# A two-layer MoE kernel: the operand sums of its last matrix product move from two engines to accumulating DMAs

## The chip, the cores and the metric

The kernel runs on one core of a Trainium2 chip. The metric is the device time of one execution, in microseconds (us). The core has a matrix engine (TensorE, PE), three engines for other arithmetic (VectorE, DVE; ScalarE, ACT; GpSimd, POOL), and SyncE (SP), which here issues transfers. Each engine takes its instructions in order. Transfers run on 16 DMA queues and may be issued from SP or POOL.

## What is computed

Attention over pooled keys and values gives `x`; two feed-forward layers follow, each with 4608 tokens, 512 model columns and 2048 inner columns:

```python
def reference(...):
    x = attn_out.transpose(0, 2, 1, 3).reshape(4608, 512)
    h = x @ moe_w_in;  x = maximum(0.01 * h, h) @ moe_w_out
    h = x @ moe2_w_in; g = where(h >= 1, h, where(h <= -1, 0, (h + 1)**2 / 4))
    return g @ moe2_w_out
# inside the attention: k and v are means over 8 rows, and
#   attn = exp(scores - max);  attn = attn / (sum(attn) + 1e-9)
```

All arrays are float32. The kernel keeps that accuracy by splitting each operand `a` into `hi` (rounded to the matrix engine's format) and `lo = a - hi`, and adding three products: hi x hi, hi x lo, lo x hi.

## The kernel before

The first layer runs in blocks of 512 tokens with the attention of later blocks woven in. The second layer's first product and its second product each use a Winograd form of Strassen's method: an operand is cut into 2 x 2 blocks, and 7 products of sums of blocks replace 8 products of blocks.

The change concerns the second product, `g @ moe2_w_out`, in `second_phase`. `g` lies in device memory, transposed, so that the inner dimension runs over partitions. A round `r` takes 1024 tokens (rounds 0 to 3; round 4 has 512) as two rows of 512 (256 in round 4), and the 2048 inner columns as two halves of 8 blocks `f`. So a block of `g` is `a11`, `a12`, `a21` or `a22`, each of 8 tiles `f` of 128 x 512. `g_load` brings them in by DMA from SP; the places are three sets of eight tiles, named `m0` to `m7`, `m8` to `m15` and so on in a listing of the program.

Within a round the seven products come in the order `ORDER2` = 4, 5, 7, 6, 1, 3, 2, each over the 8 blocks `f`. One product and one `f` is a *unit* `u`; a round has 56. A unit is 12 matmuls of 256 columns (4 groups of 128 tokens by 3), 6 in round 4. Four of the products need a sum, which `g_sum` makes in place, tile by tile: for 5, `a22 = a21 + a22`; for 7, `a21 = a11 - a21`; for 6, `a22 = a22 - a11`; for 3, `a22 = a12 - a22`. It puts even `f` on DVE and odd `f` on POOL (in round 4 all on POOL).

`hi(u)` is an ACT copy of the unit's operand and `lo(u)` a DVE subtraction. There are six pairs of tiles for them, so a pair comes free when PE has used the unit six before. The order of the work is written by hand: after the matmuls of unit `u` the program issues `hi(u + 5)`, `lo(u + 4)`, the sum for unit `u + 7`, in round 0 a fetch of product weights (`w2_fetch`, 512 KB for two `f`), the loads that reuse a place just read, and two steps of `post`. `post` copies or adds the banks of a finished product into output tiles and stores them; the additions of `q` to `r1` and `r2` there are POOL's.

Weights of the second product are split beforehand, in the first product's phase: `w2_sums` makes the sums of weight blocks on POOL, `w2_split` their `hi` (ACT) and `lo` (DVE), and a DMA puts them into device memory.

In the attention, `normalize` sums the exponentials over 64 columns and over 8 columns into two small tiles, adds them and 1e-9 with one DVE instruction, takes the reciprocal on DVE, and multiplies on POOL.

Of the kernel before, what the change touches and what calls it, by code (L numbers as in the profile page):

```python
# [17 lines left out]
P = 128  # L18
# [11 lines left out]
ORDER2 = (4, 5, 7, 6, 1, 3, 2)  # L30

# [4 lines left out]
def attention_moe_moe2(ctx: ExitStack, tc: tile.TileContext, qT, kT, v, k01, v01, w_in1, w_out1, w_in2, w_out2, out):  # L36
# [161 lines left out]
    class Attention:  # L198
        def __init__(self, apool):
            self.ap = apool  # L200
            self.sets = []
            for i in range(2):
                kp = apool.tile([P, KT, 2 * SP], F32, name=f"kp{i}", bufs=1)
                vh = apool.tile([P, KT, P], F32R, name=f"vh{i}", bufs=1)
                vl = apool.tile([P, KT, P], F32R, name=f"vl{i}", bufs=1)
                vr = apool.tile([96, KT, P], F32R, name=f"vr{i}", bufs=1)
                self.sets.append((kp, vh, vl, vr))
            self.q, self.main, self.rest, self.wide, self.raws = {}, {}, {}, {}, {}
            self.attn = {}
            self.u = None  # L210

        def zero(self):
            for kp, vh, vl, _ in self.sets:
                for t, n in ((kp, SP), (vh, D), (vl, D)):
                    nc.gpsimd.memset(t[0:64, :, n:].bitcast(F32), 0.0)
                    nc.gpsimd.memset(t[64:P, :, 0:n].bitcast(F32), 0.0)
            t = room(8, [P, 272], F32, "sums")
            self.sums = t[:, 0:176]
            self.sums_r = t[0:64, 176:272]
            nc.vector.memset(self.sums, 0.0)  # L220
            for c in (48, 112):
# [153 lines left out]
        def scores_early(self, blk, hf, ti, tag):  # L375
# [11 lines left out]
            m = self.ap.tile([P, 4, 1], F32, tag="stat", name=f"m{blk}_{hf}_{ti}", bufs=12)  # L387
# [16 lines left out]
            r = self.ap.tile([P, 4, 1], F32, tag="stat", name=f"r{blk}_{hf}_{ti}", bufs=12)  # L404
            r2 = self.ap.tile([P, 4, 1], F32, tag="stat", name=f"s{blk}_{hf}_{ti}", bufs=12)
# [6 lines left out]
        def scores(self, blk, hf, ti):  # L412
# [13 lines left out]
            m = self.ap.tile([P, 4, 1], F32, tag="stat", name=f"m{blk}_{hf}_{ti}", bufs=12)  # L426
# [4 lines left out]
            r = self.ap.tile([P, 4, 1], F32, tag="stat", name=f"r{blk}_{hf}_{ti}", bufs=12)  # L431
            r2 = self.ap.tile([P, 4, 1], F32, tag="stat", name=f"s{blk}_{hf}_{ti}", bufs=12)
# [6 lines left out]
        def normalize(self, n, main, rest, r, r2):  # L439
            nc.vector.tensor_reduce(out=r[0:n, :, 0], in_=main, axis=AX.X, op=ALU.add)  # L440
            yield True
            nc.vector.tensor_reduce(out=r2[0:n, :, 0], in_=rest, axis=AX.X, op=ALU.add)
            yield True
            nc.vector.scalar_tensor_tensor(
                out=r[0:n], in0=r[0:n], scalar=1e-9, in1=r2[0:n], op0=ALU.add, op1=ALU.add
            )
            yield True
            nc.vector.reciprocal(out=r[0:n], in_=r[0:n])  # L448
            yield True
            for t, w in ((main, MAIN), (rest, REST)):  # L450
                nc.gpsimd.tensor_tensor(out=t, in0=t, in1=r[0:n].to_broadcast([n, 4, w]), op=ALU.mult)  # L451
# [214 lines left out]
    class Second:  # L666
# [105 lines left out]
        def w2_sums(self, f):  # L772
# [6 lines left out]
            tt(out=s[:, 2], in0=b22, in1=b12, op=ALU.subtract)  # L779
# [3 lines left out]
        def w2_split(self, f, pos):  # L783
# [5 lines left out]
            self.parts(t[:, 0], t[:, 1], self.kept["w2s"][ORDER2[pos]])  # L789
# [217 lines left out]
        def g_sum(self, r, pos, f):  # L1007
            a = {w: self.a.get((r, w, f)) for w in ((1, 1), (1, 2), (2, 1), (2, 2))}
            prod = ORDER2[pos]
            tt = (nc.gpsimd if f % 2 or r == self.NPAIR2 - 1 else nc.vector).tensor_tensor  # L1010
            if prod == 5:
                tt(out=a[2, 2], in0=a[2, 1], in1=a[2, 2], op=ALU.add)
            elif prod == 7:
                tt(out=a[2, 1], in0=a[1, 1], in1=a[2, 1], op=ALU.subtract)
            elif prod == 6:
                tt(out=a[2, 2], in0=a[2, 2], in1=a[1, 1], op=ALU.subtract)
            elif prod == 3:
                tt(out=a[2, 2], in0=a[1, 2], in1=a[2, 2], op=ALU.subtract)
# [29 lines left out]
        def second_phase(self):  # L1048
# [5 lines left out]
            self.hi(4)  # L1054
            post = []
            for u, (r, pos, f) in enumerate(self.units):
# [17 lines left out]
                if u + 7 < NU:  # L1074
                    self.g_sum(*self.units[u + 7])
# [18 lines left out]
        def post(self, r, prod, n):  # L1094
# [17 lines left out]
            def snap(key, i, prod, row=None, col=None):  # L1112
                t = self.kept[key, r] = tile_of(i)
                yield
                for k in range(nb):
                    nc.scalar.activation(out=t[:, k], in_=banks(prod)[k], func=AF.Copy)
                    yield
                if row is not None:
                    store(t, row, col)

# [15 lines left out]
            def chain(*gens):  # L1136
# [9 lines left out]
                3: lambda: chain(add("q", 5, 0, 1)),  # L1146
                2: lambda: chain(snap("c11", 3, 1, 0, 0)),
# [256 lines left out]
```

## Time and profile before

| | |
|---|---|
| Median of 3 runs | 1707.95 us (1701.2 to 1708.09) |
| The profiled execution | 1704.4 us, of which the span in the profile is 1702.6 us |
| Mean granted TensorE clock | 0.991 of full speed |
| PE busy | 1660.0 us |
| DVE busy | 1086.4 us |
| ACT busy | 896.1 us |
| POOL busy | 448.0 us |
| Second product, first to last matmul | 1323.3 to 1698.8 us |

Times in the profile are microseconds from the start of the span. Busy times are sums over the whole span, and stages differ: what a stage waits for has to be read within the stage. The page's chain of waits goes back from the last instruction, at each step to what released it. "SPq" is SP issuing a transfer, which is not the time the transfer takes to land.

### The profile page before, as it was taken

To read this page: it belongs to the slowest core of one execution; us is meant where nothing else is said; L and a number is where in the kernel's file an instruction comes from. 1 tells how busy PE (TensorE), PEld (TensorE's weight loads), DVE (VectorE), ACT (ScalarE), POOL (GpSimd) and SP (SyncE) were. 2 spreads that over 40 slices of the span, in tenths; PEclk is the share of its full clock that TensorE was granted. 3 is DMA by queue.
4 is the path that set the end of the run, shared out by engine and by line. 5 is a ranking of instruction groups with operands and counts; after the bars stand their busy time and mean duration, and the time that the engine had idled before them with its cause. 6 is when DMAs were issued, how large, how long until landed. Compare 5 with 4: busy or idle time off the path is not lost.

```text
span 1702.6 us, 27338 instructions
## 1 busy us (share of the span) xinstructions
PE 1660.0 (97%) x9372; PEld 1478.9 (87%) x9372; DVE 1086.4 (64%) x2095; ACT 896.1 (53%) x1969; POOL 448.0 (26%) x552
## 2 busy tenths in 40 slices
PE   6889999999999999999999999999999799999998
PEld 4568878788888888888888899999999799999998
DVE  7868754545555455553436566775664888897967
ACT  4546543434444443443334588888886444454444
POOL 3533311211121021111114222221110434252525
PEclk9889999999999999999999999999999999999999
DMA  6424333223132322322121275576346874435231
GB/s 218 152 76 163 93 116 116 83 70 112 55 118 68 98 88 65 112 67 70 55 96 54 68 251 182 197 243 233 130 152 213 305 270 141 140 110 180 69 117 59
DMA packets 154219, 221.48 MB, mean 130 GB/s; under 512 B 18592, under 2 KB 95392, under 8 KB 154080
## 3 DMA queue, kind: packets, MB, share of 16 engines
q1 hardware_dynamic: 154080, 219.73, 39.6%
q8 instruction: 74, 1.21, 0.3%
q14 instruction: 65, 0.53, 0.1%
HBM read 136.84 MB, written 82.84 MB: 129 GB/s over the span
## 4 chain that ended last, share of the span: by engine, by line
PE 88%; DVE 5%; DMA 4%; ACT 1%; issue 1%; POOL 0%; SPq 0%; DVEq 0%; POOLq 0%; ACTq 0%
PE u L1068 20%; PE Y L837 8%; PE acc L621 8%; PE acc L622 7%; PE acc L623 7%; PE h L594 7%; PE h L595 7%; PE h L596 7%; PE X L837 5%; PE V L837 5%; PE sc L418 2%; PE tm L474 1%; DVE m L1033 1%; PE av L492 1%; PE av L494 1%
## 5 line engine op out<-in xcount | busy, mean ns | idle before, releaser
L1068 PE MATMUL u<-v,m 128*128 128x256 f32 x3024 | 367.6, 284 | 7.9 <-DVE m L1033 7.6
L1068 PEld LDWEIGHTS u<-v,m 128*128 128x128 f32 x3024 | 365.3, 193 | 10.1 <-DVE m L1033 9.3
L1033 DVE TENSOR_TENSOR m<-m,m 128x512 fp32r<-128x512 f32 (+1 forms) x280 | 249.1, 919 | 56.6 <-ACT m L1028 49.3
L1028 ACT ACTIVATE m<-m 128x512 fp32r<-128x512 f32 (+1 forms) x280 | 162.7, 588 | 190.3 <-PE u L1068 139.1
L131 DVE TENSOR_TENSOR gl<-t,gh 128x512 fp32r<-128x512 f32 x136 | 98.2, 722 | 228.8 <-ACT gh L129 223.0
L621 PE MATMUL acc<-gh,w0o 128*128 128x512 f32 x576 | 232.2, 403 | 0.0
L595 PE MATMUL h<-xl,w0i 128*128 128x512 f32 x576 | 225.8, 392 | 5.0 <-DVE xl L180 4.1
L594 PE MATMUL h<-xh,w0i 128*128 128x512 f32 x576 | 229.3, 398 | 0.6 <-DMA xh<-xk 0.6
L623 PE MATMUL acc<-gh,w0o 128*128 128x512 f32 x576 | 226.2, 393 | 0.0
L622 PE MATMUL acc<-gl,w0o 128*128 128x512 f32 x576 | 226.2, 393 | 0.0
L596 PE MATMUL h<-xh,w0i 128*128 128x512 f32 x576 | 225.6, 392 | 0.0
L605 ACT ACTIVATE t<-h 128x512 f32<-128x512 f32 x144 | 86.0, 598 | 251.1 <-PE h L596 154.1
L595 PEld LDWEIGHTS h<-xl,w0i 128*128 128x128 f32 x576 | 108.6, 189 | 27.8 <-DVE xl L180 4.9
L621 PEld LDWEIGHTS acc<-gh,w0o 128*128 128x128 f32 x576 | 109.1, 189 | 23.9 <-issue 2.4
L594 PEld LDWEIGHTS h<-xh,w0i 128*128 128x128 f32 x576 | 108.6, 189 | 23.9 <-DMA xh<-xk 1.3
L623 PEld LDWEIGHTS acc<-gh,w0o 128*128 128x128 f32 x576 | 108.8, 189 | 23.4
L596 PEld LDWEIGHTS h<-xh,w0i 128*128 128x128 f32 x576 | 108.6, 189 | 22.7
L622 PEld LDWEIGHTS acc<-gl,w0o 128*128 128x128 f32 x576 | 109.3, 190 | 20.9
L451 POOL TENSOR_TENSOR at<-at,r 128x32 f32<-128x32 f32 (+3 forms) x160 | 67.9, 445 | 136.4 <-DVE r L448 117.4
L129 ACT ACTIVATE gh<-t 128x512 fp32r<-128x512 f32 x144 | 91.0, 632 | 4.4
L837 PE MATMUL Y<-xs,v 128*128 128x384 f32 x432 | 86.3, 336 | 1.3 <-DVE p L856 0.7
L837 PE MATMUL X<-xs,v 128*128 128x384 f32 x432 | 86.5, 334 | 0.0
(269 smaller groups left out, 2874.0 us busy)
## 6 DMA issues: line engine op xcount, KB each, us to landing
m<-g SPq DMA_DIRECT2D x128, 256.0 KB
w2d<-w2o SPq DMA_DIRECT2D x56, 256.0 KB
v<-w2d SPq DMA_DIRECT2D x28, 512.0 KB
x<-o SPq DMA_DIRECT2D x36, 256.0 KB
xr<-x SPq DMA_DIRECT2D x24, 384.0 KB
g<-tX SPq DMA_DIRECT2D x48, 192.0 KB
g<-tV SPq DMA_DIRECT2D x48, 192.0 KB
g<-tW SPq DMA_DIRECT2D x48, 192.0 KB
```

What stands on the lines that cost most here:

```text
L129: nc.scalar.activation(out=hi, in_=src, func=AF.Copy)
L131: engine.tensor_tensor(out=lo, in0=src, in1=hi, op=ALU.subtract)
L594: nc.tensor.matmul(ph, wh[:, c], xh, start=k == 0, stop=False)
L595: nc.tensor.matmul(ph, wh[:, c], xl, start=False, stop=False)
L596: nc.tensor.matmul(ph, wl[:, c], xh, start=False, stop=k == KT - 1)
L621: nc.tensor.matmul(acc, wh[:, c], gh, start=st, stop=False)
L622: nc.tensor.matmul(acc, wh[:, c], gl, start=False, stop=False)
L623: nc.tensor.matmul(acc, wl[:, c], gh, start=False, stop=sp)
L837: nc.tensor.matmul(ps, w[:, c], x[k, i], start=begin and k == n == 0, stop=k == 1 and n == 2, skip_group_check=True,)
L1028: nc.scalar.activation(out=self.s[u][0], in_=self.unit_source(u), func=AF.Copy)
L1033: nc.vector.tensor_tensor(out=lo, in0=self.unit_source(u), in1=hi, op=ALU.subtract)
L1068: nc.tensor.matmul(ps, a[:, c], w, start=begin and i == 0, stop=f == self.NJ - 1 and i == 2, skip_group_check=True,)
```

## The change

The sums of `g` blocks are made by DMAs that POOL issues, from SBUF to SBUF, which add the source to what lies at the target. Such a DMA can only add, so the signs move: the first row of blocks is treated as its negative, and the minus signs go into the weights of products 1, 2 and 3, into the weight sum for product 7, and into the two outputs of the first row. The sum for unit `u + 10` is issued where that for `u + 7` was (`AHEAD2 = 10`), and the first ten before the loop.

In the attention, the two partial sums and a constant 1e-9 lie in the three columns of one small tile (two such tiles alternate), and one reduction over the columns joins them.

```diff
+DEN = 2
+AHEAD2 = 10
+            self.parts3 = [apool.tile([P, 4, 3], F32, name=f"ds{i}", bufs=1) for i in range(DEN)]
+            for t in self.parts3:
+                nc.vector.memset(t[:, :, 2:3], 1e-9)
...
         def normalize(self, n, main, rest, r, r2):
-            nc.vector.tensor_reduce(out=r[0:n, :, 0], in_=main, axis=AX.X, op=ALU.add)
+            nc.vector.tensor_reduce(out=r2[0:n, :, 0], in_=main, axis=AX.X, op=ALU.add)
             yield True
-            nc.vector.tensor_reduce(out=r2[0:n, :, 0], in_=rest, axis=AX.X, op=ALU.add)
+            nc.vector.tensor_reduce(out=r2[0:n, :, 1], in_=rest, axis=AX.X, op=ALU.add)
             yield True
-            nc.vector.scalar_tensor_tensor(
-                out=r[0:n], in0=r[0:n], scalar=1e-9, in1=r2[0:n], op0=ALU.add, op1=ALU.add
-            )
+            nc.vector.tensor_reduce(out=r[0:n, :, 0], in_=r2[0:n], axis=AX.X, op=ALU.add)
...
-            tt(out=s[:, 2], in0=b22, in1=b12, op=ALU.subtract)
+            tt(out=s[:, 2], in0=b12, in1=b22, op=ALU.subtract)
...
-            self.parts(t[:, 0], t[:, 1], self.kept["w2s"][ORDER2[pos]])
+            x = self.kept["w2s"][ORDER2[pos]]
+            if ORDER2[pos] < 4:
+                nc.scalar.activation(out=t[:, 0], in_=x, func=AF.Copy, scale=-1.0)
+                nc.vector.scalar_tensor_tensor(
+                    out=t[:, 1], in0=x, scalar=-1.0, in1=t[:, 0], op0=ALU.mult, op1=ALU.subtract
+                )
+            else:
+                self.parts(t[:, 0], t[:, 1], x)
...
-        def g_sum(self, r, pos, f):
...
+        def g_sum(self, u):
+            if not 0 <= u < len(self.units):
+                return
+            r, pos, f = self.units[u]
+            to, more = {
+                5: ((2, 2), (2, 1)), 7: ((2, 1), (1, 1)), 6: ((2, 2), (1, 1)), 3: ((2, 2), (1, 2))
+            }.get(ORDER2[pos], (None, None))
+            if to:
+                nc.gpsimd.dma_start(out=self.a[r, to, f], in_=self.a[r, more, f], accum_op=ALU.add)
...
+            for u in range(AHEAD2):
+                self.g_sum(u)
...
-                if u + 7 < NU:
-                    self.g_sum(*self.units[u + 7])
+                self.g_sum(u + AHEAD2)
...
+            def add_minus(key, prod, row, col):
+                t = self.kept[key, r]
+                for k in range(nb):
+                    nc.vector.scalar_tensor_tensor(
+                        out=t[:, k], in0=banks(prod)[k], scalar=-1.0, in1=t[:, k], op0=ALU.mult, op1=ALU.subtract
+                    )
...
-                3: lambda: chain(add("q", 5, 0, 1)),
-                2: lambda: chain(snap("c11", 3, 1, 0, 0)),
+                3: lambda: chain(add_minus("q", 5, 0, 1)),
+                2: lambda: chain(snap("c11", 3, 1, 0, 0, -1.0)),
```

The order of the instructions changes on three engines at the start of the second phase. POOL first, in round 0: in the kernel before these are the sums for product 5 (L1012) and 7 (L1014), for odd `f` (`m0` to `m7` is `a22`, `m8` on is `a21`; a number after the last underscore only tells allocations apart).

```order
L1012 TENSOR_TENSOR m1_13222<-m9_13277,m1_13222 128x512 [waits DMAHW1_49,DMAHW7_49,DVE_49,PE_49]
L1012 TENSOR_TENSOR m3_13226<-m11_13281,m3_13226 128x512 [waits DMAHW3_49,DVE_49,PE_49]
L1012 TENSOR_TENSOR m5_13239<-m12_13303,m5_13239 128x512 [waits DMAHW7_49,DVE_49,PE_49]
L1012 TENSOR_TENSOR m7_13243<-m15_13307,m7_13243 128x512 [waits DMAHW5_49,DMAHW1_49,DVE_49]
L1014 TENSOR_TENSOR m9_13277<-m15_13307,m9_13277 128x512 [waits DMAHW6_49,PE_49,Pool_49]
```

In the changed kernel the same place on POOL holds a DMA for every `f`.

```order
L1030 DMA m0_13144<-m8_13199 128x512 [waits DMAHW0_49,DMAHW6_49,DVE_49,PE_49]
L1030 DMA m1_13146<-m9_13201 128x512 [waits DMAHW7_49,DMAHW1_49,DVE_49]
L1030 DMA m2_13148<-m10_13203 128x512 [waits DMAHW2_49,DVE_49,PE_49]
L1030 DMA m3_13150<-m11_13205 128x512 [waits DMAHW3_49,DVE_49]
L1030 DMA m4_13161<-m12_13227 128x512 [waits DMAHW6_49,DVE_49,PE_49]
L1030 DMA m5_13163<-m12_13227 128x512 [waits DMAHW7_49,DVE_49]
L1030 DMA m6_13165<-m12_13227 128x512 [waits DMAHW4_49,DMAHW0_49,DVE_49]
L1030 DMA m7_13167<-m15_13231 128x512 [waits DMAHW5_49,DMAHW1_49,DVE_49]
L1030 DMA m8_13199<-m15_13231 128x512 [waits DMAHW5_49,DMASW0_49,PE_49]
```

The tensor operations of POOL are gone; the ninth DMA waits (DMASW0) for the landing of the first.

On ACT, the `hi` of units 7 to 11 in the kernel before: from unit 8 on they read sums.

```order
L1028 ACTIVATE m21_13298<-m7_13243 128x512 [waits DVE_49,PE_49]
L1028 ACTIVATE m24_13310<-m0_13220 128x512 [waits DVE_49,PE_49]
L1028 ACTIVATE m32_13342<-m1_13222 128x512 [waits PE_49,Activation_49,Pool_49]
L1028 ACTIVATE m34_13346<-m2_13224 128x512 [waits DVE_49,PE_49,Activation_49]
L1028 ACTIVATE m30_13363<-m3_13226 128x512 [waits PE_49,Activation_49,Pool_49]
```

The same in the changed kernel:

```order
L1040 ACTIVATE m21_13222<-m7_13167 128x512 [waits DVE_49,PE_49]
L1040 ACTIVATE m24_13234<-m0_13144 128x512 [waits DMASW0_49,DVE_49,PE_49]
L1040 ACTIVATE m32_13266<-m1_13146 128x512 [waits DMASW1_49,DVE_49,PE_49]
L1040 ACTIVATE m34_13270<-m2_13148 128x512 [waits DMASW2_49,DVE_49,PE_49]
L1040 ACTIVATE m30_13289<-m3_13150 128x512 [waits DMASW3_49,DVE_49,PE_49]
```

The order of the copies is the same; from unit 8 on each waits for the landing of a DMA.

On DVE, `lo` of units 4 to 9 in the kernel before, with the first sums between them:

```order
L1033 TENSOR_TENSOR m35_13347<-m4_13237,m34_13346 128x512
L1033 TENSOR_TENSOR m31_13364<-m5_13239,m30_13363 128x512
L1012 TENSOR_TENSOR m0_13220<-m8_13275,m0_13220 128x512
L1033 TENSOR_TENSOR m21_13298<-m6_13241,m21_13298 128x512
L1033 TENSOR_TENSOR m24_13310<-m7_13243,m21_13298 128x512
L1012 TENSOR_TENSOR m2_13224<-m10_13279,m2_13224 128x512
L1033 TENSOR_TENSOR m24_13310<-m0_13220,m24_13310 128x512
L1033 TENSOR_TENSOR m33_13343<-m1_13222,m32_13342 128x512
```

The same in the changed kernel:

```order
L1045 TENSOR_TENSOR m35_13271<-m4_13161,m34_13270 128x512
L1045 TENSOR_TENSOR m31_13290<-m5_13163,m30_13289 128x512
L1045 TENSOR_TENSOR m21_13222<-m6_13165,m21_13222 128x512
L1045 TENSOR_TENSOR m24_13234<-m7_13167,m21_13222 128x512
L1045 TENSOR_TENSOR m24_13234<-m0_13144,m24_13234 128x512
L1045 TENSOR_TENSOR m33_13267<-m1_13146,m32_13266 128x512
```

The sums have left DVE; the subtractions follow each other.

## Rows read from the trace of the kernel before

**Rows 1.** The page's busy times: us, share of the span, instructions.

```profile
PE 1660.0 (97%) x9372; PEld 1478.9 (87%) x9372; DVE 1086.4 (64%) x2095; ACT 896.1 (53%) x1969; POOL 448.0 (26%) x552
```

**Rows 2.** Chain of waits, second phase: start, length, what held it.

```profile
1330.37 5.06 DMA g<-tY
...
1351.65 326.76 PE u L1068 x2716
...
1679.21 19.58 PE u L1068 x160
```

**Rows 3.** Timeline of PE: start, length, operation, [idle before and its releaser].

```profile
1323.30 4.81 PE L1068 MATMUL u<-v,m 128*128 128x256 f32 x36
...
1329.09 3.38 PE L1068 MATMUL u<-v,m 128*128 128x256 f32 x24 [0.22 <-DVE m L1033]
1336.29 8.95 PE L1068 MATMUL u<-v,m 128*128 128x256 f32 x60 [3.81 <-DVE m L1033]
1346.58 3.39 PE L1068 MATMUL u<-v,m 128*128 128x256 f32 x24 [1.34 <-DVE m L1033]
1351.65 2.54 PE L1068 MATMUL u<-v,m 128*128 128x256 f32 x19 [1.68 <-DVE m L1033]
...
1679.21 3.02 PE L1068 MATMUL u<-v,m 128*128 128x256 f32 x23 [0.59 <-DVE m L1033]
```

**Rows 4.** Groups by line: busy us, mean ns, idle before and its releasers.

```profile
L1033 DVE TENSOR_TENSOR m<-m,m 128x512 fp32r<-128x512 f32 x224 | 214.2, 981 | 48.2 <-ACT m L1028 41.0 <-DMA g<-tY 4.8
...
L1014 POOL TENSOR_TENSOR m<-m,m 128x512 f32<-128x512 f32 x16 | 27.4, 1743 | 0.0
...
L1012 POOL TENSOR_TENSOR m<-m,m 128x512 f32<-128x512 f32 x16 | 24.3, 1523 | 115.6 <-DMA m<-g 71.3 <-DVE m L1033 44.3
...
L1012 DVE TENSOR_TENSOR m<-m,m 128x512 f32<-128x512 f32 x16 | 19.7, 1230 | 0.0
```

**Rows 5.** Stretches: length, busy of PE/PEld/DVE/ACT/POOL, granted clock, DMA share, GB/s.

```profile
1330.00:1351.00 21.00, 14.81 (x103) 13.80 (x101) 16.19 (x13) 6.58 (x12) 15.28 (x10) 0.92 1.03 396
1357.00:1393.00 36.00, 36.00 (x302) 36.00 (x302) 29.93 (x44) 17.51 (x29) 6.63 (x4) 1.00 0.87 307
...
1336.00:1339.00 3.00, 2.71 (x12) 2.71 (x13) 3.00 (x4) 1.15 (x2) 1.62 (x1) 0.55 1.06 403
...
1412.00:1493.00 81.00, 81.00 (x677) 81.00 (x676) 69.21 (x81) 38.97 (x65) 32.25 (x20) 1.00 0.42 132
```

**Rows 6.** Timeline of SP's issues; L999 is `g_load`, L966 `w2_fetch`.

```profile
1336.09 6.73 SPq L966 DMA_DIRECT2D v<-w2d  x9
1357.43 0.32 SPq L999 DMA_DIRECT2D m<-g  x1
...
1365.23 4.18 SPq L966 DMA_DIRECT2D v<-w2d  x5
```

**Rows 7.** Timeline of DVE and POOL at the start of round 0.

```profile
1335.55 0.69 DVE L1033 TENSOR_TENSOR m<-m,m 128x512 fp32r<-128x512 f32 x1 [4.81 <-DMA g<-tY]
...
1328.70 3.18 POOL L1012 TENSOR_TENSOR m<-m,m 128x512 f32<-128x512 f32 x2 [69.74 <-DMA m<-g]
```

**Rows 8.** Timeline of POOL, round 4: first and last of 8 sums for product 5.

```profile
1650.05 0.74 POOL L1012 TENSOR_TENSOR m<-m,m 128x256 f32<-128x256 f32 x1 [6.45 <-DVE m L1033]
...
1659.75 0.85 POOL L1012 TENSOR_TENSOR m<-m,m 128x256 f32<-128x256 f32 x1 [0.41 <-POOL m L1012]
```

**Rows 9.** Group by line: the instruction that joined the denominator.

```profile
L444 DVE SCALAR_TENSOR_TENSOR r<-r,s 128x4 f32<-128x4 f32 x64 | 14.8, 231 | 1.6
```

**Rows 10.** The page's DMA issues: transfer, issuer, count, KB each.

```profile
m<-g SPq DMA_DIRECT2D x128, 256.0 KB
...
v<-w2d SPq DMA_DIRECT2D x28, 512.0 KB
```

More of the change, by code (lines that the diff above doesn't have):

```diff
@@ L210, in __init__ @@
             self.u = None
+            self.parts3 = [apool.tile([P, 4, 3], F32, name=f"ds{i}", bufs=1) for i in range(DEN)]
+            self.n_den = 0
         def zero(self):
+            for t in self.parts3:
+                nc.vector.memset(t[:, :, 2:3], 1e-9)
             for kp, vh, vl, _ in self.sets:
@@ L386, in scores_early @@
             sc = ps[0:n, 0:4 * SP].rearrange("p (h k) -> p h k", h=4)
-            m = self.ap.tile([P, 4, 1], F32, tag="stat", name=f"m{blk}_{hf}_{ti}", bufs=12)
+            m = self.ap.tile([P, 4, 1], F32, tag="stat", name=f"m{blk}_{hf}_{ti}", bufs=8)
             nc.vector.tensor_reduce(out=m[0:n, :, 0], in_=sc, axis=AX.X, op=ALU.max)
@@ L403, in scores_early @@
             yield True
-            r = self.ap.tile([P, 4, 1], F32, tag="stat", name=f"r{blk}_{hf}_{ti}", bufs=12)
-            r2 = self.ap.tile([P, 4, 1], F32, tag="stat", name=f"s{blk}_{hf}_{ti}", bufs=12)
+            r = self.ap.tile([P, 4, 1], F32, tag="stat", name=f"r{blk}_{hf}_{ti}", bufs=8)
+            r2 = self.parts3[self.n_den % DEN]
+            self.n_den += 1
             parts = self.normalize(n, main, rest, r, r2)
@@ L425, in scores @@
             self.attn[hf, ti] = a
-            m = self.ap.tile([P, 4, 1], F32, tag="stat", name=f"m{blk}_{hf}_{ti}", bufs=12)
+            m = self.ap.tile([P, 4, 1], F32, tag="stat", name=f"m{blk}_{hf}_{ti}", bufs=8)
             yield True
@@ L430, in scores @@
             scale = 1.0 / (POOL * D**0.5)
-            r = self.ap.tile([P, 4, 1], F32, tag="stat", name=f"r{blk}_{hf}_{ti}", bufs=12)
-            r2 = self.ap.tile([P, 4, 1], F32, tag="stat", name=f"s{blk}_{hf}_{ti}", bufs=12)
+            r = self.ap.tile([P, 4, 1], F32, tag="stat", name=f"r{blk}_{hf}_{ti}", bufs=8)
+            r2 = self.parts3[self.n_den % DEN]
+            self.n_den += 1
             nc.vector.tensor_tensor(out=sc, in0=sc, in1=m[0:n].to_broadcast([n, 4, SP]), op=ALU.subtract)
@@ L1005, in pair2 @@
             return (1024 * r, 512) if r < self.NPAIR2 - 1 else (1024 * r, 256)
-        def g_sum(self, r, pos, f):
[L1008 to L1018, printed above, removed]
+        def g_sum(self, u):
[7 more added lines that the diff above has]
+                nc.gpsimd.dma_start(out=self.a[r, to, f], in_=self.a[r, more, f], accum_op=ALU.add)
         def unit_source(self, u):
@@ L1110, in store, with snap @@
                 )
-            def snap(key, i, prod, row=None, col=None):
+            def snap(key, i, prod, row=None, col=None, scale=1.0):
                 t = self.kept[key, r] = tile_of(i)
@@ L1115, in snap @@
                 for k in range(nb):
-                    nc.scalar.activation(out=t[:, k], in_=banks(prod)[k], func=AF.Copy)
+                    nc.scalar.activation(out=t[:, k], in_=banks(prod)[k], func=AF.Copy, scale=scale)
                     yield
@@ L1119, in snap @@
                     store(t, row, col)
+            def add_minus(key, prod, row, col):
[4 more added lines that the diff above has]
+                    )
+                    yield
+                store(t, row, col)
             def add(key, prod, row=None, col=None):
```

## The prediction

> **What bounds the kernel now.** I read the page's busy times first. TensorE (PE) is busy for 97% of the span [rows 1], so work that leaves another engine gains time only where PE waits for that engine. Next I read the chain of waits in the second layer's second product (the second phase): one unbroken stretch of PE from 1351.65 on, 326.76 us for 2716 matmuls, or 0.1203 us each [rows 2]. A unit (one product, one block of 128 rows of the contraction, 512 tokens) is 12 matmuls, so 1.444 us; in the last round, with 256 tokens, 0.722 us. The sums that the change moves are wholly hidden inside that stretch. What is left to gain lies at its two ends.
>
> The timeline of PE shows them [rows 3]. In round 0 PE stops three times: 3.81 us before unit 5, 1.34 us before unit 10, and 1.68 us before unit 12; in the last round once, for 0.59 us. All four waits are for DVE's `lo`. The first is not DVE's own work: DVE itself waits 4.81 us for the store `g<-tY` [rows 7], whose tile `lo(5)` writes; the chain has that store at 5.06 us [rows 2], behind a full queue. The 1.34, the 1.68 and the 0.59 are DVE's work: a `lo` takes 0.98 us in the mean, a sum of product 5 on DVE 1.23 us, a sum on POOL 1.5 us or more [rows 4]. [...]
>
> **Sums off DVE and POOL.** 64 sums leave DVE and 96 leave POOL. That takes away the 1.34 and the 1.68, so 3.0 us in round 0, and the 0.59 in the last round. Nothing else on PE waits for them. They come back as 160 DMAs, which all wait in POOL's queue (for the `lo` that read the target, for the loads, and for the sum eight units earlier). Behind a sum that waits stand the later sums and the additions of `q`; ACT's `hi` now waits for the landing, and behind it on ACT stand the later `hi` and the copies out of the banks, behind those DVE's `lo`, and then PE. SP's next loads wait for the sums that read their place. The lead is long: six pairs of `hi` and `lo` tiles let a `lo` run about four units ahead of PE, and a sum waits for the `lo` eight units before its own, so it can start about 12 units, 17 us, before PE needs it.
>
> **What a sum costs the DMA queues.** The trace has no such transfer. While the queues are full they move 396 GB/s [rows 5], so 256 KB [rows 10] take 0.66 us. A load is one read and one write of that size; a sum is two reads and a write. The bounds are therefore one transfer, 0.66 us, and three, 1.97 us. I take two, 1.31 us, as a load already pairs a read with a write and one read is added. [...]
>
> **Round 0, first collision.** POOL's first sum in the trace starts at 1328.70, when its loads are in [rows 7]. Five sums (targets f = 0 to 4) can be issued before the store `g<-tY` lands at 1335.43. They share the queues with it, so it lands 5 x 0.66 = 3.3 to 5 x 1.31 = 6.6 us later, and the 3.81 us stop grows by that. At the low end this just cancels the 3.0 us that DVE gives back: +0.3 us.
>
> **Round 0, balance of the queues.** The queues are busy from 1330 to 1351.3 already, with nine weight tiles of 512 KB issued from 1336.09 [rows 5, 6, 10], and at 0.87 of 36 us after 1357. Weights of the product that begins with unit 48 (the 25th tile, last of the five issued from 1365.23 [rows 6]) have ahead of them 21.3 us to 1351.3, then three tiles and eight loads (3.9 + 5.2 us), then five tiles (6.6 us): 37.0 us. With 31 sums after 1330 at 1.31 us, 40.6 us, the tile lands at 1330 + 77.6 = 1407.6. PE reaches unit 48 in the trace at 1351.65 + 36 x 1.444 = 1403.6. So PE is 4.0 us later there, and this contains the first collision and the 3.0 us. At 0.66 us a sum the same line gives 1387, and nothing waits. So round 0 is +0.3 to +4.0 us; I take +4.0.
>
> **Rounds 1 to 3.** A round of 81 us has the queues busy for 0.42, 34 us [rows 5]. 32 sums at 1.31 us add 42: 76 of 81. The loads are 14 units ahead and the sums 12, so I put this at nothing. Its cover is thin: it is gone from (81 - 34)/32 = 1.47 us a sum.
>
> **Last round.** Units are half as long, but POOL must issue as many sums. In the trace its last sum of product 5 starts at 1659.75, the first at 1650.05 [rows 8]; 16 more follow without a pause. Unit 31 is the last that needs one of these. PE ends at 1698.79 [rows 2], 25 units of 0.722 us before that is 1680.7, and without the 0.59 it is 1680.1. So its sum must have landed by 1679.1 (`hi` and `lo` need about a us). What issuing costs on POOL no row shows. Below is SP's issue of the same tile, 0.32 us [rows 6]; above, POOL's own sum, 1.74 us [rows 4]. I take the middle, 1.03, and 3 us to land (under the 5.06 us behind a full queue): 1659.75 + 17 x 1.03 + 3 = 1680.3, a wait of 1.2 us in place of 0.59, so +0.6. Up to 0.96 us there is none, -0.6; at 1.74 us it is 13.2, +12.6.
>
> **The rest.** In the denominator one instruction of 231 ns [rows 9] becomes a sum over three columns. 18 of the 64 lie in the first blocks, where PE waits for the attention. Between nothing and 18 x 0.231 = 4.2 us; I take -1.0, a quarter, as an instruction remains in its place. Two small memsets at the start run while the first loads are on their way. Negated weights are the same count of instructions of the same size on ACT and DVE in the first phase, where PE never waits for `w2_split`; negated outputs likewise: nothing.
>
> **Sum.** +4.0 + 0.6 - 1.0 = +3.6 us on the profiled run's 1704.4 (its span of 1702.6 and 1.8 around it): 1708.0. The median of the runs, 1707.95, lies 3.55 us above that run, so I state 1711.6.
>
> **Rivals.** (1) *The sums are dearer to the queues* than 1.47 us, and PE waits for sums in every round. At 1.6 us each: 32 x 1.6 + 34 = 85, so 4 us in each of three rounds, and in round 0 37.0 + 31 x 1.6 gives 1416.6, 13 us late: about 12 + 13 - 0.4 = +25, 1733. At 1.97 us: 16 a round and 24.5, some +72, 1780. For it: the small margin. Against it: reads and writes need not share a limit. (2) *Issuing is dear on POOL*, above 0.96 us, felt in the last round alone: at 1.74 us 12 more than forecast, 1723.6. For it: POOL's own operations on this tile take that long, and those on DVE are drawn out beside them. [...] (3) *No collision*: the sums start late enough, or cost 0.66 us, and the store is not held up: -3.0 - 0.6 - 1.0 = -4.6, 1703.4. [...] (4) That the sums stay on an engine cannot be: the built program has 160 DMAs there.
>
> **Chances.** Forecast 0.42. Rival 3 0.20, of which 0.07 beyond 0.5%. Rival 1 0.20, rival 2 0.18, both mostly slower by over 0.5%. So faster 0.07, same 0.55, slower 0.38. The range, 1702 to 1738, takes in rival 3 but for its end, rival 2, and rival 1 up to 1.6 us; about 0.18 is left out.
>
> **What would show it.** DVE's wait for `g<-tY` grows from 4.81 to 8 or more; no stops of PE for DVE's work in units 10 to 12; the queues' share near 0.9 in rounds 1 to 3; `lo` at 0.69 us instead of 0.98; PE late at units 40 to 48, waiting for weights or sums; a wait of about a us near unit 31 of the last round; POOL's DMAs near 1 us. A share near 0.7 would say that a sum is one transfer; PE waiting for `hi` in every round is rival 1; only in the last, rival 2. Wrong outright would be a PE pace that differs from 0.1203 us.

## The result, and the profile after

The changed kernel takes 1714.91 us (median of 7 runs, 1712.46 to 1718.14) against 1707.76 us for the kernel before (7 runs): a ratio of 1.0054, 95% interval 1.0037 to 1.0071, so about 9 us slower (0.0054 x 1707.76). The profiled run took 1712.46 us, its span is 1710.7. The time is within the range, 3.3 us above the forecast of 1711.6. The rest of this document shows that the forecast came so near because two of its terms were wrong in opposite directions, which is luck.

The timeline of TensorE (PE) of the changed kernel over the second layer's second product (the second phase), start, length, operation, idle before and releaser, answers to [rows 3]. `lo` is L1045 now, `hi` L1040, the matmuls L1082:

```profile
1315.04 4.79 PE L1082 MATMUL u<-v,m 128*128 128x256 f32 x36
...
1320.82 3.13 PE L1082 MATMUL u<-v,m 128*128 128x256 f32 x24 [0.23 <-DVE m L1045]
1332.16 21.04 PE L1082 MATMUL u<-v,m 128*128 128x256 f32 x154 [8.22 <-DVE m L1045]
1354.07 0.50 PE L1082 MATMUL u<-v,m 128*128 128x256 f32 x2 [0.87 <-ACT m L1040]
1354.80 1.46 PE L1082 MATMUL u<-v,m 128*128 128x256 f32 x10 [0.22 <-DVE m L1045]
...
1384.88 74.09 PE L1082 MATMUL u<-v,m 128*128 128x256 f32 x612 [0.22 <-DVE m L1045]
...
1461.13 225.78 PE L1082 MATMUL u<-v,m 128*128 128x256 f32 x1866 [0.22 <-DVE m L1045]
1687.33 19.45 PE L1082 MATMUL u<-v,m 128*128 128x256 f32 x160 [0.42 <-DVE m L1045]
```

Three things are to be seen. The stop before unit 5 grew from 3.81 to 8.22 us. The stops for VectorE's work before units 10 and 12, 1.34 and 1.68 us, are gone, but the 154 matmuls after the long stop take 21.04 us, 0.137 each instead of 0.1203, and from 1354.07 to 1384.88 PE stops in every unit: 158 matmuls, some 13 units, take 30.8 us, 2.34 us a unit instead of 1.444. From 1384.88 on PE runs almost without a break, as before. From the phase's first matmul to the stop of the last round it is 355.91 us before (1323.30 to 1679.21) and 372.29 after: 16.4 us longer. Some 14 us of it are lost by 1384.88, where 31 units are done (69.84 us after the phase's start, against 28.35 us for 12 units and 19 more at 1.444 us before); some 2 us follow in round 1, of which below. But the phase also begins 8.3 us earlier, at 1315.04 instead of 1323.30. That gain and that loss make the result.

What VectorE (DVE) and ScalarE (ACT) waited for around round 0: in us in total, times, longest. The first line answers to [rows 7].

```profile
DVE m L1045 <- DMA g<-tY: 10.0, 1, 10.0
...
ACT m L1040 <- DMA m<-m: 36.3, 21, 3.2
```

The store held `lo(5)` 10.0 us, where it was 4.81. `hi` then waited 36.3 us for sums to land (`m<-m` are the accumulating DMAs), which no engine did before.

The stretches answer to [rows 5]: length, busy of PE, PEld, DVE, ACT, POOL (GpSimd), granted clock, DMA share, GB/s.

```profile
1325.00:1335.00 10.00, 2.84 (x13) 2.84 (x14) 3.59 (x6) 2.40 (x4) 2.60 (x4) 0.61 1.10 274
...
1355.00:1365.00 10.00, 7.62 (x48) 5.99 (x47) 2.76 (x4) 3.49 (x6) 3.45 (x4) 1.00 1.08 297
...
1405.00:1486.00 81.00, 80.33 (x660) 79.23 (x659) 44.62 (x65) 38.06 (x63) 33.53 (x36) 1.00 1.04 272
...
1567.00:1648.00 81.00, 81.00 (x677) 81.00 (x677) 46.11 (x65) 39.29 (x65) 35.27 (x37) 1.00 0.93 215
```

The queues are full through round 0, counted at 1.08 to 1.10, yet move only 268 to 305 GB/s in each 10 us from 1325 to 1395, where [rows 5] has 396. In the stretch from 1405 to 1486, most of which is round 1, PE ran 660 matmuls where the kernel before ran 678, so some 2 us went there: between 1453 and 1475 weight loads and matmuls waited for `lo` in seven places (2.1 us), and `hi` for sums in six (6.8 us). PE's granted clock was 0.61 in the 10 us around the long stop. Of the 154 matmuls behind the stop, 14 ran in the first 3 us at a granted clock of 0.50, 18 in the next 3 us at 0.62, and 27 in the 3 us after that at 1.00. The page's row on the software queue (packets, MB, share of 16 queues), in which the sums run, and its group of their issues:

```profile
q0 software_dynamic: 23040, 37.76, 12.5%
...
L1030 POOL DMA_DIRECT2D m<-m x160 | 139.8, 1216 | 214.6 <-DMA m<-g 94.0
```

The group of `lo`, by form, answers to [rows 4]:

```profile
L1045 DVE TENSOR_TENSOR m<-m,m 128x512 fp32r<-128x512 f32 x224 | 162.6, 739 | 159.4 <-ACT m L1040 144.8 <-DMA g<-tY 10.0 <-PE u L1082 3.0
```

The 128 sums of 256 KB and 32 of 128 KB are 144 of the full size; 12.5% of 1710.7 us over 144 is 1.49 us of all queues for one. `lo` fell from 981 to 739 ns in the mean.

### The profile page after: what moved, and what is told of

The parts are those of the page before. It is cut to its first block, busy times and chain, and to the rows that moved or that the text cites. A ratio compares the mean times of both kernels' runs of the same rounds, so it can differ in the third digit from the quotient of the medians.

```text
span 1710.7 us, 27456 instructions
## 1 busy us (share of the span) xinstructions
PE 1663.8 (97%) x9372; PEld 1479.0 (86%) x9372; DVE 976.9 (57%) x2033; ACT 896.1 (52%) x1969; POOL 458.7 (27%) x616
## 3 DMA queue, kind: packets, MB, share of 16 engines
q0 software_dynamic: 23040, 37.76, 12.5%
## 4 chain that ended last, share of the span: by engine, by line
PE 81%; DMA 9%; DVE 4%; issue 2%; ACT 1%; POOL 1%; SPq 0%; POOLq 0%; DVEq 0%; ACTq 0%
PE u L1082 14%; PE Y L852 8%; PE acc L629 7%; PE acc L630 7%; PE acc L631 7%; PE h L602 7%; PE h L603 7%; PE h L604 7%; PE X L852 5%; PE V L852 5%; DMA m<-m 4%; PE sc L427 2%; DMA m<-g 1%; PE tm L482 1%; DMA wb0i<-in_moe_w_in_dram 1%
## 5 line engine op out<-in xcount | busy, mean ns | idle before, releaser
L1082 PE MATMUL u<-v,m 128*128 128x256 f32 x3024 | 375.6, 285 | 16.2 <-DVE m L1045 12.4
L1082 PEld LDWEIGHTS u<-v,m 128*128 128x128 f32 x3024 | 367.7, 193 | 24.0 <-DVE m L1045 17.7
L1045 DVE TENSOR_TENSOR m<-m,m 128x512 fp32r<-128x512 f32 (+1 forms) x280 | 187.3, 684 | 178.1 <-ACT m L1040 162.2
L1040 ACT ACTIVATE m<-m 128x512 fp32r<-128x512 f32 (+1 forms) x280 | 161.8, 587 | 206.5 <-PE u L1082 130.0
L1030 POOL DMA_DIRECT2D m<-m x160 | 139.8, 1216 | 214.6 <-DMA m<-g 94.0
## 6 DMA issues: line engine op xcount, KB each, us to landing
m<-m POOLq DMA_DIRECT2D x128, 256.0 KB, 11.1
```

What stands on the lines that cost most here:

```text
L1030: nc.gpsimd.dma_start(out=self.a[r, to, f], in_=self.a[r, more, f], accum_op=ALU.add)
L1040: nc.scalar.activation(out=self.s[u][0], in_=self.unit_source(u), func=AF.Copy)
L1045: nc.vector.tensor_tensor(out=lo, in0=self.unit_source(u), in1=hi, op=ALU.subtract)
L1082: nc.tensor.matmul(ps, a[:, c], w, start=begin and i == 0, stop=f == self.NJ - 1 and i == 2, skip_group_check=True,)
```

## The experiments

Ratios are to the kernel before, timed beside each run on the same chip, with their 95% intervals. Products 5, 7, 6 and 3 need the sums, and round 0 has 32 of them.

**e1: everything but the DMAs.** The sums are additions on VectorE and GpSimd again.

```diff
-                nc.gpsimd.dma_start(out=self.a[r, to, f], in_=self.a[r, more, f], accum_op=ALU.add)
+                t, m = self.a[r, to, f], self.a[r, more, f]
+                e = nc.gpsimd if f % 2 or r == self.NPAIR2 - 1 else nc.vector
+                e.tensor_tensor(out=t, in0=m, in1=t, op=ALU.add)
...
-                self.g_sum(u + AHEAD2)
+                self.g_sum(u + 7)
```

> Everything of the change but its accumulating DMAs: the sums stand on VectorE and GpSimd again, seven units ahead as before, now as plain additions; the moved signs and the new denominators stay. Theory A (the change holds two effects: the DMAs cost the second phase the 16.3 us by which it is longer in the trace after, 391.8 against 375.5, and the denominators and signs give back the 8.3 us by which the part ahead is shorter): 1707.8 - 8.3 = about 1699.5 us, the second phase's first product near 1315, the stop of TensorE before unit 5 back near 3.8 us. Rival B (the 8.3 us ahead of the second phase are the spread of single runs, the denominators give nothing): 1707 to 1708 us.

Measured: 1698.94 us, ratio 0.9972 (0.9962 to 0.9982). Theory A holds: the DMAs alone cost 1.0054 - 0.9972 = 0.0082, 14 us, and what is left of the change gains about 5. PE's timeline at the phase's start and at the last round's stop:

```profile
1316.24 5.45 PE L1082 MATMUL u<-v,m 128*128 128x256 f32 x38
...
1672.97 19.55 PE L1082 MATMUL u<-v,m 128*128 128x256 f32 x160 [0.59 <-DVE m L1047]
```

Between the two lie 356.73 us, 15.6 less than in the changed kernel. The stop before unit 5 is 4.73 us, not 3.8, with no DMA sum beside it.

**e2: the DMAs with the old denominators.** The edit also puts back the small tiles of the old form and their 12 buffers, of which the changed kernel has 8.

```diff
...
-            nc.vector.tensor_reduce(out=r[0:n, :, 0], in_=r2[0:n], axis=AX.X, op=ALU.add)
+            nc.vector.scalar_tensor_tensor(
+                out=r[0:n], in0=r[0:n], scalar=1e-9, in1=r2[0:n], op0=ALU.add, op1=ALU.add
+            )
...
```

> The DMAs with the signs, and the denominators of the kernel before (the join of two sums with its constant by one instruction, stat tiles of 12 buffers). Theory A: the 8.3 us of the first part are lost and the DMAs' cost is paid: 1714.9 + 8.3 = about 1723 us, the second phase's first product near 1323. Rival B: as the changed kernel, 1714 to 1716 us.

Measured: 1720.91 us, 1.0104 (1.0084 to 1.0124), 0.0050 or 8.5 us more than the changed kernel. The second phase began at 1321.21. Theory A again, from the other side.

**e3: plain copies.** The transfers stay; the sums of the four products are left out.

```diff
-                ..., in_=self.a[r, more, f], accum_op=ALU.add)
+                ..., in_=self.a[r, more, f])
```

> The same DMAs at the same places without the accumulation: plain copies, so that the operand sums of products 5, 7, 6 and 3 are left out. Theory A1 (the price is the reading of the destination): a transfer of 256 KB takes near 0.66 us of all queues (the 396 GB/s at which loads ran in the trace before) in place of the 1.49 us worked out from the trace after (12.5% of 1710.7 us over 144 transfers of 256 KB); round 0 loses little by the queues, and the time falls by 4 to 12 us, to 1703 to 1711 us. Rival A2 (the price is the place of the transfers in the order, ahead of the store and the weights, whatever they do there): within 2 us of the changed kernel, 1713 to 1717 us.

Measured: 1697.02 us, 0.9953 (0.9936 to 0.9969), a larger gain than A1 had given; A2 falls. Its software queue on the page:

```profile
q0 software_dynamic: 11776, 37.76, 6.1%
```

Its PE from unit 5 to the end, in one piece:

```profile
1331.35 358.39 PE L1082 MATMUL u<-v,m 128*128 128x256 f32 x2962 [7.12 <-DVE m L1045]
```

Two of its stretches, columns as above:

```profile
1355.00:1365.00 10.00, 10.00 (x86) 10.00 (x85) 6.98 (x12) 4.42 (x7) 1.07 (x2) 1.00 1.03 394
...
1405.00:1486.00 81.00, 81.00 (x677) 81.00 (x677) 45.95 (x65) 39.41 (x65) 24.33 (x37) 1.00 0.72 237
```

A copy of 256 KB takes 6.1% x 1693.7 / 144 = 0.72 us of all queues, a sum 1.49: 2.07 times as much. The bytes counted are the same, the packets twice as many (23040 and 11776), so the price goes with the accumulation; whether it is the reading of the destination, as A1 had it, or the smaller packets, this run doesn't tell. The stop before unit 5 is still 7.12 us, but there are no stops behind it.

**e4: round 0 on the engines, the later rounds by DMA.**

```diff
+            if (r == 0) != first:
+                return
...
-                self.g_sum(u + AHEAD2)
+                self.g_sum(u + 7, True)
+                self.g_sum(u + AHEAD2, False)
```

> The 32 sums of the first round stand on VectorE and GpSimd, seven units ahead as before; the sums of the rounds 1 to 3 and of the last round stay DMAs. Theory A (the loss is the first round's: 8.2 us of stop and the slow clock behind it, then the small stops to 1385 us, while the later rounds hide the DMAs): the 16.3 us go all but some 2 us, 1714.9 - 14 = about 1701 us. Rival C (the DMAs' load is spread, and every round pays a part of it): 1708 to 1713 us.

Measured: 1698.47 us, 0.9961 (0.9946 to 0.9977); Theory A, not C. PE's timeline from unit 12 on:

```profile
1347.10 327.38 PE L1086 MATMUL u<-v,m 128*128 128x256 f32 x2718 [1.68 <-DVE m L1051]
1675.03 19.46 PE L1086 MATMUL u<-v,m 128*128 128x256 f32 x160 [0.56 <-DVE m L1051]
```

The second round, as a stretch:

```profile
1405.00:1486.00 81.00, 81.00 (x678) 81.00 (x677) 45.80 (x65) 39.33 (x65) 35.16 (x37) 1.00 0.98 239
```

128 of the 160 DMAs run here and PE's stretch is as unbroken as in [rows 2]. So the whole loss of 14 to 16 us comes from round 0's 32 DMAs, the 2 us in round 1 too: this kernel ran 678 matmuls from 1405 to 1486. The 128 DMAs gained nothing that shows either (e1, without them, is at 0.9972). A round's share rose from 0.42 [rows 5] to 0.98, so a sum costs 0.56 x 81 / 32 = 1.42 us there; in e3 it is 0.30 x 81 / 32 = 0.76 us a copy.

**e5: the kernel before with the new denominators alone.** The diff is that of the change for the denominators, and nothing else.

> The kernel before with the new denominators alone (three columns, one TENSOR_REDUCE; stat tiles of 8 buffers). Theory P (the denominators alone are the gain ahead of the second phase, since VectorE's join of two SBUF operands was held up by GpSimd, 577 ns a piece between 20 and 130 us of the trace before, against 164 ns for the reduction after): 16 x (577 - 164) ns = 6.6 us at most, of which the two runs that differ by it have shown 4.8 and 6.0 us: ratio to the kernel before 0.996 to 0.9975, some 1700 us. Rival S (the moved signs or the order of the second phase have a part in it): ratio 0.998 to 1.000.

Measured: 1697.5 us, 0.9959 (0.9944 to 0.9975). Theory P: the denominators are the whole gain, 4 to 9.5 us by the interval, and the moved signs (in e1, not here) cost nothing that shows; a cost of some 2 us, the difference of the two ratios, would not show.

**e6: e1 with a join that reads two operands.**

```diff
-            nc.vector.tensor_reduce(out=r[0:n, :, 0], in_=r2[0:n], axis=AX.X, op=ALU.add)
+            nc.vector.scalar_tensor_tensor(
+                out=r[0:n], in0=r2[0:n, :, 0:1], scalar=1e-9, in1=r2[0:n, :, 1:2], op0=ALU.add, op1=ALU.add
+            )
```

> The kernel of e1_sums_on_engines with one instruction changed: the join reads two columns of the new tile by a scalar_tensor_tensor with two SBUF inputs, as before, in place of the reduction over three columns; tiles, buffers and signs stay. Theory P (two SBUF inputs are held up while GpSimd works): the join takes near 1 us in about half of its places between 20 and 130 us again, mean over 500 ns there, and the time goes back by 4 to 6 us to 1703 to 1705 us. Rival T (the new tiles and the buffer counts brought the gain): the time stays at 1698 to 1700 us.

Measured: 1704.62 us, 0.9999 (0.9988 to 1.0010): the gain is gone with one instruction changed back, so it is not from the tiles and buffers. The profiled runs agree: the phase began at 1321.2 to 1323.3 us in the three with the old join (the kernel before, e2, e6) and at 1315.0 to 1319.5 in the ten with the new one. The means differ by 4.9 us, so a part of the 8.3 us of the first pair of traces was the spread of single runs. The group by line between 20 and 130 us (busy us, mean ns, idle), of the kernel before:

```profile
L444 DVE SCALAR_TENSOR_TENSOR r<-r,s 128x4 f32<-128x4 f32 (+1 forms) x16 | 9.2, 577 | 0.5
```

Of the changed kernel:

```profile
L454 DVE TENSOR_REDUCE r<-ds 128x4 f32<-128x12 f32 (+1 forms) x16 | 2.6, 164 | 0.8
```

Of e6:

```profile
L454 DVE SCALAR_TENSOR_TENSOR r<-ds 128x4 f32<-128x4 f32 (+1 forms) x16 | 10.1, 633 | 0.8
```

Why 577 ns, for an instruction that takes 160 ns elsewhere, is in the timeline of DVE of the kernel before (start, length):

```profile
98.91 0.17 DVE L442 TENSOR_REDUCE s<-at 128x4 f32<-128x32 f32 x1
99.12 1.07 DVE L444 SCALAR_TENSOR_TENSOR r<-r,s 128x4 f32<-128x4 f32 x1
```

And in that of its POOL:

```profile
98.89 1.28 POOL L119 TENSOR_TENSOR wc0i<-wc0i,wb0i 128x512 uint32<-128x512 uint32 x1 [1.84 <-DVE wc0i L115]
```

GpSimd's operation ran from 98.89 to 100.17. The reduction, one input, started after it and took 0.17 us, as all 16 between 20 and 130 us did (0.167 to 0.178). The join, two inputs, started at 99.12 and ended at 100.19, 0.02 us after GpSimd's. The same is seen at 24.03, 35.13 and 53.30. Seven of the 16 joins took 0.98 us or more. Three of the seven lie between 20 and 64 us, where VectorE hardly pauses (busy for 20.50 of the 22 us from 20 to 42 and 20.93 of the 22 from 42 to 64), the others where it has more room (16.82 of the 21 us from 64 to 85). At these four times the join ended 0.01 to 0.02 us after GpSimd's operation, so the wait is the remainder of that operation; what holds the join up for that time no run shows.

**e7: the changed kernel with the halves of unit 5 in another place.**

```diff
-                    pool, tag = {..., 30: (g_p, "gh"), 31: (g_p, "gh")}.get(
+                    pool, tag = {..., 30: (raw_p, "raw"), 31: (raw_p, "raw")}.get(
```

> The changed kernel with one place moved: the operand halves of the units 5, 11, 17 ... lie in two buffers of the input pool that is idle in the second phase, in place of the two that the last store of the first phase (tY) still reads. Theory W (the wait for the store is a cost of its own: 8.2 us of stop before unit 5 and the slow clock behind it): 1714.9 - 8 = about 1707 us or a little less. Rival Q (the DMA queues set the first round: what is not lost before unit 5 is lost behind it, since the same sums, loads and weights have to pass): at most 2 us gained, 1713 to 1715 us, with longer stops between units 10 and 40.

Measured: 1714.05 us, 1.0058 (1.0041 to 1.0074): nothing gained, rival Q. PE's timeline:

```profile
1321.42 7.78 PE L1082 MATMUL u<-v,m 128*128 128x256 f32 x60 [0.22 <-DVE m L1045]
...
1350.72 13.87 PE L1082 MATMUL u<-v,m 128*128 128x256 f32 x96 [6.05 <-DMA v<-w2d]
```

The 8.22 us stop has gone, and a stop of 6.05 us for weights stands before unit 16, with small stops at nearly every unit from 8 to 15 before it and from 24 to 30 behind it. So in the changed kernel the long stop before unit 5 was a symptom of full queues and no cost of its own.

**e8: e1 with the same place moved.**

> The kernel of e1_sums_on_engines with the same place moved. Theory W: its stop of 4.7 us before unit 5 goes, with some of the slow clock behind it (60 matmuls took 9.73 us there against 7.2 at full clock): 1698.9 - 5 = about 1694 us. Rival N (the next thing is as late: the stops before units 10 and 12 grow by what is saved): 1697 to 1699 us.

Measured: 1694.87 us, 0.9939 (0.9924 to 0.9954), 5.6 us better than e1. PE's timeline:

```profile
1325.28 5.08 PE L1082 MATMUL u<-v,m 128*128 128x256 f32 x36 [0.22 <-DVE m L1047]
1330.98 6.32 PE L1082 MATMUL u<-v,m 128*128 128x256 f32 x48 [0.62 <-DVE m L1047]
1338.96 3.38 PE L1082 MATMUL u<-v,m 128*128 128x256 f32 x24 [1.67 <-DVE m L1047]
1344.02 326.96 PE L1082 MATMUL u<-v,m 128*128 128x256 f32 x2718 [1.67 <-DVE m L1047]
```

Where the queues have room (a share of 0.79 from 1325 to 1405 in the kernel before, whose sums are on the engines too, against 1.09 in the changed kernel), the same edit gives back what it should (Theory W); the stop before unit 10 grew, so part of rival N is true.

**e9: e8 with half of round 0 as DMAs.** Even units by DMA, odd units on GpSimd, in round 0 alone.

```diff
+            if dma != (r == 0 and f % 2 == 0):
+                return
...
+                if dma:
+                    nc.gpsimd.dma_start(out=t, in_=m, accum_op=ALU.add)
+                    return
...
-                self.g_sum(u + 7)
+                self.g_sum(u + AHEAD2, True)
+                self.g_sum(u + 7, False)
```

> The kernel of e8_engines_other_place, in whose first round the sums of the even units are accumulating DMAs (issued 10 units ahead) and those of the odd units stand on GpSimd; all other rounds stand on the engines. Theory Q (a sum takes some 1.45 us of all queues, and the first round's loss is what its transfers exceed the queues by): in the kernel before the queues are busy for 63.5 of the 80 us from 1325 to 1405; 32 sums add 46 us, which is 30 too many, 16 add 23, which is 7 too many, and what is 7 too many can wait for the free queues of the second round; VectorE's stops before units 10 and 12 (1.67 us each) go as well: 1692 to 1697 us. Rival D (any accumulating DMA beside the loads and weights of the first round costs in proportion): half of the 14 to 16 us that the 32 cost, 1701 to 1703 us.

Measured: 1702.06 us, 0.9975 (0.9961 to 0.9989). The number is rival D's; the trace tells another story. PE's stop:

```profile
1346.65 6.67 PE L1089 MATMUL u<-v,m 128*128 128x256 f32 x36 [8.36 <-DVE m L1052]
```

VectorE's `lo` between 1336 and 1360 (ns: minimum, median, maximum):

```profile
L1052 DVE TENSOR_TENSOR m<-m,m x12: 675/677/9324, 1337.3 to 1359.3; 128x512 fp32r<-128x512 f32 x12
```

POOL's timeline:

```profile
1337.50 1.56 POOL L1037 TENSOR_TENSOR m<-m,m 128x512 f32<-128x512 f32 x1
1338.73 1.16 POOL L1034 DMA_DIRECT2D m<-m  x1
1339.34 1.84 POOL L1037 TENSOR_TENSOR m<-m,m 128x512 f32<-128x512 f32 x1
```

One subtraction took 9.32 us, from 1337.3 to 1346.6, while GpSimd went from sum to DMA issue to sum without a pause; another, begun between 1349 and 1351, took 5.15 us. PE's stop of 8.36 us ended with the first of them. Whether it is the cause, or only fills a time in which sums had not landed, e11 tests.

**e10: more load on the queues in rounds 1 to 3.**

```diff
                     nc.gpsimd.dma_start(out=t, in_=m, accum_op=ALU.add)
+                    if r < self.NPAIR2 - 1:
+                        nc.gpsimd.dma_start(
+                            out=self.extra[f][:, 512 * pos:512 * pos + 512], in_=self.g[f][:, 0:512]
+                        )
```

> The kernel of e4_round0_on_engines with one more transfer of 256 KB beside each sum in the rounds 1 to 3, a plain copy between two places of the device's memory that nobody reads. In e4 the queues are busy for 0.98 of 81 us a round, 79.4 us, of which the sums take 79.4 - 34 = 45.4, 1.42 us each. Theory Q (beyond 81 us a round the queues set the time): at some 0.75 us for such a copy a round needs 79.4 + 24 = 103 us, 22 us more than it has, three times: 1698.5 + 60 to 67 = 1758 to 1766 us. Rival L (TensorE is covered by the issue ahead, ten units, whatever the queues carry): 1698 to 1702 us.

Measured: 1731.06 us, 1.0154 (1.0133 to 1.0176): rival L falls, Theory Q is right in kind and half in size. The stop of PE with which the small stops of a round begin, in two rounds:

```profile
1442.17 0.50 PE L1091 MATMUL u<-v,m 128*128 128x256 f32 x2 [0.65 <-ACT m L1050]
...
1533.37 0.50 PE L1091 MATMUL u<-v,m 128*128 128x256 f32 x2 [0.77 <-ACT m L1050]
```

A stretch of 81 us:

```profile
1405.00:1486.00 81.00, 76.27 (x591) 72.97 (x590) 35.14 (x54) 32.96 (x56) 48.36 (x67) 0.98 1.09 301
```

A round takes 91.2 us instead of 81. In it the queues are counted at 1.09, not at 1.00: the share can go above one. So a round carries 81 x 1.09 = 88 us of such work, and the extra copy took (91.2 x 1.09 - 79.4) / 32 = 0.62 us by that count, not 0.75.

**e11: e9 with the other half on VectorE.**

```diff
-                e = nc.gpsimd if f % 2 or r == self.NPAIR2 - 1 else nc.vector
+                e = nc.gpsimd if r and (f % 2 or r == self.NPAIR2 - 1) else nc.vector
```

> The kernel of e9_half_of_round0 with the 16 sums of the first round's odd units on VectorE in place of GpSimd. In e9 one subtraction of VectorE took 9.3 us (0.69 elsewhere) while GpSimd ran its sums back to back, and TensorE stood for 8.4 us. Theory P (that stop is VectorE held up by GpSimd's sums, and the 16 DMAs fit in the queues): the subtraction takes 0.69 us again, the stop goes, 1702 - 8 = about 1694 us, between 1692 and 1697. Rival D (the 16 DMAs and their landing are the cost, and the long subtraction only fills a time in which data was missing anyway): 1700 to 1703 us.

Measured: 1693.39 us, 0.9932 (0.9914 to 0.9951), Theory P. PE's timeline:

```profile
1331.92 11.53 PE L1089 MATMUL u<-v,m 128*128 128x256 f32 x94 [0.22 <-DVE m L1052]
1344.27 0.50 PE L1089 MATMUL u<-v,m 128*128 128x256 f32 x2 [0.82 <-ACT m L1047]
...
1348.37 318.27 PE L1089 MATMUL u<-v,m 128*128 128x256 f32 x2646 [0.22 <-DVE m L1052]
```

A stretch of round 0:

```profile
1355.00:1365.00 10.00, 10.00 (x85) 10.00 (x85) 8.15 (x14) 5.38 (x11) 0.71 (x1) 1.00 1.06 343
```

With 16 sums by DMA the queues are counted at 1.06, and the longest stop of PE in round 0 is 0.82 us. e11 and e8 are the fastest of all, ahead of both kernels; the two can't be told apart.

## Why the prediction came out as it did

**The bound, and the pace.** Right. PE's pace held (0.1204 us a matmul, 327.38 us for 2718 in e4); apart from the slow clock behind the long stop (0.50 to 0.62 in 6 us), PE lost time in stops alone. But the stops did not stay at the two ends: they went on to 1385 and came again in round 1.

**Sums off VectorE and GpSimd.** Right: the 1.34 and 1.68 us stops went, the 0.59 became 0.42.

**The price of a sum.** Two transfers, 1.31 us, was near: 1.49 over the span, 1.42 in rounds 1 to 3, and 0.72 to 0.76 for a copy, 1.9 to 2.1 times. Two reads and a write a sum was the author's count; no run shows the reads apart.

**The first collision.** Right by itself: DVE's wait for the store grew by 5.2 us (10.0 against 4.81; by 4.3 against the 5.7 of e1), between the 3.3 and 6.6 given, PE's stop by 4.4. But e7 showed that this stop is no term of the sum: without it the queues take the time back later.

**The balance of round 0.** This is the first step that failed: +4.0 us taken, at most +4.0 allowed, 14 to 16 measured (the changed kernel against e1 and e4). The line followed one weight tile, unit 48's, and asked what stands ahead of it. With 1.49 us a sum it gives 37.0 + 31 x 1.49 = 83.2, so 1413.2 against 1403.6: 9.6 us. The rest is that PE did not wait for weights at unit 48 but for sums, in each of the units 18 to 30, from 1354 to 1385: `hi` needs its own sum's landing, and each sum stands behind whatever else the full queues hold (11.1 us from issue to landing in the median for 256 KB; e3's copies had 5.0). The count that fits is that of the whole stretch. The kernel before and the changed kernel, columns as above:

```profile
1325.00:1405.00 80.00, 72.68 (x580) 71.26 (x579) 67.85 (x80) 34.91 (x60) 32.98 (x20) 0.98 0.79 287
```

```profile
1325.00:1405.00 80.00, 66.47 (x479) 61.35 (x480) 33.45 (x50) 28.58 (x49) 27.08 (x30) 0.94 1.09 296
```

Before, the queues are busy for 63.5 of these 80 us (added up by eight stretches of 10 us, with shares from 1.06 down to 0.49); 32 sums at 1.45 add 46, together 110, where 80 x 1.09 = 87 can pass. The 23 us too many went into 16 of delay, and the rest into round 1, whose share is 1.04 where e4 has 0.98. With 16 sums it is 63.5 + 23 = 87, which just fits, and e11 lost nothing that shows. The 1.09 was read off after the runs, so the count is fitted and the limit not measured by itself; e9 and e11 were forecast with such a count and 80 us, and e11's time bears it out.

**Rounds 1 to 3.** Their own sums cost nothing (e4), as forecast; the 2 us of round 1 in the changed kernel are left over from round 0. But the margin was argued wrongly. The price of 1.42 to 1.49 lies at the 1.47 from which rival 1 was to bite, with no stop. Since the count goes to 1.09, the cover lasts to (88 - 34) / 32 = 1.7 us a sum; e10 went beyond it and paid.

**The last round.** 23 issues took 20.42 us, 0.89 each, where 1.03 was taken; the wait is 0.42 us, so -0.2 in place of +0.6. Rival 2 falls.

**The denominator.** The second step that failed: -1.0 taken, -4.2 the bound. The runs give -4.6 (e6 against e1) to -8.5 us (the changed kernel against e2), -7 for it alone (e5). [rows 9] gave one mean, 231 ns, for 64 instructions, and I took it for the duration of each. It was a mixture of 0.16 us and of 1 us, the long ones all before 110 us. (The prediction's 18 joins in the first blocks are 18 of all 80, with those on 64 rows, and not of the 64 on 128 rows.) The stretch from 20 to 130 us alone has 16 x (577 - 164) ns = 6.6 us; what the runs give beyond that is within their intervals. Minimum, median and maximum of that line would have shown it:

```profile
L444 DVE SCALAR_TENSOR_TENSOR r<-r,s x80: 145/161/1103, 14.7 to 855.1; 128x4 f32<-128x4 f32 x64, 64x4 f32<-64x4 f32 x16
```

**The signs.** Nothing that shows: e1 has them and e5 does not, 0.9972 and 0.9959 with overlapping intervals. No run has a transfer that subtracts.

**The sum.** +3.6 forecast; the runs have +7.2 by the medians and +9 by the ratio. The chances leaned to no change, 0.55 within 0.5%, which is where the forecast stood; the ratio of 1.0054 lies just beyond, with an interval across that limit. Behind it stand a loss of some 15 us and 5 to 8 that the denominators paid back, and neither was foreseen.

## What to carry to other kernels

Before work is moved to DMA queues, count the queues' busy time over the whole stretch in which they are already full, here at about twice a copy's price for an accumulating transfer (1.49 us against 0.72 for 256 KB, e3). Where there was room, the move of 128 sums cost nothing that shows, and gained nothing (e4, 0.98 of the queues' time in a round). Where there was none, 32 sums cost 14 to 16 us, and curing the first stop only shifted it (8.22 us before unit 5, then 6.05 before unit 16, e7). Read the spread of a short instruction's duration, not its mean: a two-operand VectorE instruction beside GpSimd work took 1.07 us (at 99.12) where its median is 0.16, and the one-operand form that does the same was worth more (0.9959 by itself, e5) than the large edit beside it (0.0082 lost by the DMAs, e1).

## What the runs showed of the hardware that was not expected

- In the kernel before, a VectorE instruction with two operands ended 0.02 us after the GpSimd operation that was running when it began (99.12 + 1.07 against 98.89 + 1.28), and three others 0.01 to 0.02 us after theirs; a reduction with one operand was not held up (0.17 us, in the same operation's time).
- Under GpSimd operations without a pause one such subtraction took 9.32 us instead of 0.69 and another 5.15 (e9). The first is recorded from 1337.27, during a DMA issue and 0.23 us before the next sum, and ended only when five sums and five issues more had begun; why not after the first of them is open, and GpSimd's recorded times overlap (a sum from 1337.50 to 1339.06, the next issue from 1338.73).
- The share of the queues is counted at 1.10 while accumulating transfers run, at 274 GB/s (the changed kernel, 1325 to 1335), and at 1.03 with 394 GB/s of plain copies (e3): a higher share is not more data. Nor need a share near one stop the engines: at 0.98 over a round PE lost nothing (e4, 678 matmuls in 81 us, as before).
- GpSimd's issue of an accumulating DMA took 0.86 us in the median of 160 (the changed kernel), that of a plain copy of the same tile 0.54 (e3).
